# Four and three buffers for a weight conversion, and the second batch's attention products in plain float32

## The chip, the cores and the metric

The kernel runs on one core of a Trainium2 chip. The metric is the device time of one execution in microseconds (us). Three runs of the kernel before took 2249.56, 2252.94 and 2246.89 us; the median is 2249.56 us.

The engines are named as the profile names them: PE (TensorE, matmuls and transposes), PEld (its weight loads), DVE (VectorE), ACT (ScalarE), POOL (GpSimd) and SP (SyncE, which here issues every DMA). PSUM is the memory that PE writes; it is used in banks of 128 x 512 float32.

## What is computed

For 8 batches of 448 tokens with 12 heads of 64, the reference computes an attention, a spectral mix and a feed-forward block:

```python
q_n, k_n = rmsnorm(q, g_q), rmsnorm(k, g_k)
scores = q_n @ k_n.T / 8                      # 448 x 448 per head
attn = exp(scores - max) / (sum + 1e-9)
x = concat_heads(attn @ v)                    # 448 x 768 per batch
u = x + real(fft(fft(x, axis=tokens), axis=features))
un = (u - mean) / sqrt(var + 1e-6)
out = u + relu(un @ w_ch1) @ w_ch2            # 768 -> 3072 -> 768
```

The weights come as 64-bit floats and everything else as float32. The kernel reads each 64-bit number as two 32-bit words and makes two float32r numbers of it (float32r is the rounded kind that PE multiplies in fewer passes): a high part and the small rest.

## The kernel before, in words

**Two numbers for one.** A precise product is made of float32r matmuls: an operand is split into a rounded value and the rest, and two or three matmuls are summed. The split costs an ACT copy (the rounded value) and a DVE subtraction (the rest). The alternative, called plain here, feeds the float32 tile to PE as it is. A plain matmul appears in the trace as two PE records; a float32r one is one record.

**Attention of one pair of heads** (`transpose_pair`, `softmax_pair`, `value_pair`). q and k of a pair are normalised and transposed. Split, this leaves QT and KD, and the rests in the upper half of QT and in `rounded` (KL); plain, it leaves two tiles, head 0 in partitions 0 to 63 and head 1 in 64 to 127. The scores are made in four chunks of 112 rows, each head into its own PSUM bank: split, two matmuls per head (line 348); plain, one with 64 rows (line 345). After the softmax the chunks P are transposed into `pt` (line 392 plain, 420 split), copied to T, and multiplied with v into `av`, which is copied to xT. Split, v is vhl (an ACT copy and a POOL subtraction), T is split by ACT and DVE, a head needs seven matmuls (lines 432 and 437), and xT is put together by an ACT copy and a DVE addition. Plain, a head needs four matmuls (lines 399 and 403) into 64 partitions of `av`, and one copy.

Which pairs are plain stands in two ranges over the number 6 x batch + pair: the values of `PLAIN_PAIRS` and the scores of `PLAIN_SCORES`. Before, these are pairs 0 to 5 and 2 to 5, all of batch 0.

**Feed-forward** (`ffn`). `up(m)` makes one of 24 hidden tiles with 18 matmuls (line 851), `down(g, d)` one of 36 partial outputs with 12 (line 872): 864 matmuls for a batch. Each uses one weight tile of `Stream` W1 or W2, which keeps three tiles loaded and asks for the next when one was used.

**Conversion of the weights** (`convert`, `Stream.converted`). In the first pass a weight tile is loaded as 64-bit words into `dbl`, worked on, and stored to DRAM as its two float32r parts, from where the other seven batches load it. One tile is one DMA load (line 651), two ACT operations (654 and 655), three DVE operations (656, 660 and 664), a POOL addition (668), an ACT copy (669), a POOL subtraction (670) and a DMA store (700). The loaded words lie in a buffer of the tag X, the work in one of the tag M; there are two of each. 14 tiles are converted beside the attention of batch 0, the other 46 during the feed-forward of batch 0.

**Order.** `merge` interleaves the feed-forward of batch b with attention and spectral mix of batch b+1, by nominal costs that each step yields. So batch 1's attention and the 46 conversions run beside batch 0's feed-forward. A scheduler then sets the order on each engine, and every engine, SP included, works through its queue in that order. Reuse of a buffer waits for the last reader of what was in it.

Of the kernel before, what the change touches and what calls it, by code (L numbers as in the profile page):

```python
# [13 lines left out]
U32 = mybir.dt.uint32  # L14
U64 = mybir.dt.uint64
AF = mybir.ActivationFunctionType
# [3 lines left out]
B, H, S, D = 8, 12, 448, 64  # L20
DM = H * D
DFF = 4 * DM
C = 112
NC = S // C
NPAIR = H // 2
NR = DM // 128
# [15 lines left out]
CONVERT_EARLY = 0.12  # L42
EARLY = 2
DFT_STEP = 40
PLAIN_PAIRS = range(NPAIR)
PLAIN_SCORES = range(2, NPAIR)
PACE = 3
LAG = 3

# [39 lines left out]
def spectral_block(ctx, tc, q, k, v, g_q, g_k, w1, w2, d1, d2, out, nb=B):  # L89
# [49 lines left out]
    def bank(tag, name):  # L139
        if tag == "either":  # L140
            tag = ("q", "av")[turn[0] % 2]
            turn[0] += 1
        return ps.tile([128, 512], F32, tag=tag, name=name, bufs=BANKS[tag])
# [3 lines left out]
    def slot(tag, name, dtype=F32):  # L147
        return sb.tile([128, 900], dtype, tag=tag, name=name, bufs=SLOTS[tag])

    def wide(name, dtype=F32):  # L150
        return sb.tile([128, 1800], dtype, tag="X", name=name, bufs=2)
# [179 lines left out]
    def softmax_pair(b, p, Pc):  # L331
        QT, KD, _ = ready[b, p]
        for c in range(NC):
# [39 lines left out]
            Pc.append(P)  # L373
            yield 760

    def value_pair(b, p, Pc, xT):
        vhl = ready[b, p][2]
        rem = bank("PT", f"rem{b}_{p}")
# [4 lines left out]
        if plain(b, p):  # L383
            R = slot("PT", f"R{b}_{p}")[:, :S]
            A.copy(R, rem[:, :S])
            yield 420
            for h, a in enumerate((lo, hi)):
                av = bank("either" if b == 0 else "av", f"av{b}_{p}_{h}")
                for j in range(3):
                    pt = bank("PT", f"pt{b}_{p}_{h}_{j}")  # L390
                    for c in range(NC):
                        nc.tensor.transpose(
                            pt[:, c * C : (c + 1) * C],
                            Pc[c][:, 512 * h + j * 128 : 512 * h + (j + 1) * 128],
                            ident[:C, :C],
                        )
                    T = slot("PT", f"T{b}_{p}_{h}_{j}")[:, :S]
                    A.copy(T, pt[:, :S])
                    nc.tensor.matmul(
                        av[:D, :S], vhl[:, j, h], T, start=j == 0, stop=False  # L400
                    )
                    yield 1180
                nc.tensor.matmul(
                    av[:D, :S], vhl[a, 3, h], R[a], start=False, stop=True
                )
                A.copy(xT[a, p, :S], av[:D, :S])
                yield 760
            A.copy(xT[:, p, S : S + 1], xT[:, p, 0:1])
            return
# [233 lines left out]
    def convert(src, bits, part, name):  # L643
# [1 line left out]


        _, c, f = src.shape
        raw = wide(f"dbl{name}", U32)[:, : c * f].rearrange(
            "r (c f w) -> r c f w", c=c, w=2
        )  # L650
        nc.sync.dma_start(raw.rearrange("r c f w -> r c (f w)"), src)
        low, high = raw[:, :, :, 0], raw[:, :, :, 1]
        value = bits.bitcast(F32)
        behind(nc.scalar.activation(value, high.bitcast(F32), AF.Abs))
        behind(nc.scalar.activation(low, low, AF.Copy, scale=2.0**-29))
        behind(nc.vector.tensor_scalar(
            out=value, in0=value, scalar1=MIN_HIGH, scalar2=MAX_HIGH,
            op0=ALU.max, op1=ALU.min,
# [15 lines left out]
    class Stream:  # L674
# [18 lines left out]
        def converted(self, i, name):  # L693
            hl = self.tile(name)
            src = self.doubles(i)
            bits = slot("M", f"mag{self.tag}{name}", U32)[:, : self.n * 128].rearrange(
                "r (c f) -> r c f", c=self.n
            )
            convert(src, bits, [hl[:, k] for k in range(2)], f"{self.tag}{name}")
            nc.sync.dma_start(self.kept(i), hl.bitcast(F32))  # L700
            return hl
# [231 lines left out]

# [19 lines left out]
```

## Time and profile before

| | |
|---|---|
| median of three runs | 2249.56 us (2246.89 to 2252.94) |
| span of the profiled execution, first to last instruction | 2245.4 us |
| busy share of the span: PE, DVE, ACT, POOL | 94%, 72%, 47%, 24% |
| mean granted TensorE clock | 0.963 of 2.4 GHz |
| DMA moved | 425.32 MB, mean 189 GB/s |

The page gives the profiled execution's span and no time of its own beside it; the median of the runs lies 4.2 us above that span. The page cuts the span into 40 slices of about 56 us. Batch 0's attention and spectral mix fill the first 196 us; batch 0's feed-forward runs from there to about 555 us; from 555 us on each batch takes about 249 us (the 48 spectral matmuls of line 531 come at 757.28, 1006.05, 1255.05 and 1503.73 us in the chain of waits). A busy share is an average over stages with different limits, so the windows by stage below say more than the table.

### The profile page before, as it was taken

The page shows a single profiled execution, that of the slowest core. Times are in us where ns is not written, and L with a number is a line of the kernel's source. Part 1 is how long each engine was busy: PE and PEld are TensorE (multiplying, and loading weights), DVE is VectorE, ACT ScalarE, POOL GpSimd, SP SyncE. Part 2 cuts the span into 40 slices and gives each one's busy share as a digit, 9 for nine tenths or more (in the row PEclk, how much of TensorE's full clock was granted, in tenths as well). Part 3 has the DMA queues.
Part 4 walks back from the last instruction along what each step waited for, and adds up shares of the span by engine and source line. Part 5 has one row for each costly group of instructions (what it writes and reads, how often), then busy time and mean ns, then how long its engine had stood idle before and what let it go on. Part 6 is the DMA issues. An engine that isn't in the chain of part 4 may idle for free.

```text
span 2245.4 us, 31410 instructions
## 1 busy us (share of the span) xinstructions
PE 2112.2 (94%) x11164; PEld 1858.3 (83%) x11164; DVE 1617.8 (72%) x3083; ACT 1061.0 (47%) x2290; POOL 536.4 (24%) x322
## 2 busy tenths in 40 slices
PE   7877877788999999999999999999999999999997
PEld 3336766667999999999999999999999999998996
DVE  7887899877688577876888577866788587753122
ACT  6856776454454255534554255524554355422100
POOL 5763556455122012210122021211121022000000
PEclk7988988888999999999999999999999999999999
DMA  5556445577755575556655575557655675549664
GB/s 154 163 171 216 154 156 185 175 255 250 215 176 168 188 238 167 174 189 199 204 172 180 188 226 166 176 177 226 188 170 177 207 215 162 176 137 281 213 207 134
DMA packets 298238, 425.32 MB, mean 189 GB/s; under 512 B 186545, under 2 KB 224418, under 8 KB 298082
## 3 DMA queue, kind: packets, MB, share of 16 engines
q1 hardware_dynamic: 298082, 423.32, 60.4%
q8 instruction: 89, 1.46, 0.3%
q14 instruction: 67, 0.55, 0.1%
HBM read 363.47 MB, written 65.27 MB: 191 GB/s over the span
## 4 chain that ended last, share of the span: by engine, by line
PE 78%; DVE 10%; ACT 3%; DMA 3%; issue 3%; POOL 2%; SPq 0%; DVEq 0%; POOLq 0%; ACTq 0%
PE h L851 28%; PE o L872 28%; PE S L348 5%; PE av L432 4%; PE pt L420 4%; PE y L531 2%; DMA dblw<-w 2%; PE qk L311 1%; DVE mn L112 1%; DVE P L112 1%; DVE eo L112 1%; ACT P L112 1%; POOL magw L668 1%; PE oT L817 1%; DVE magw L664 1%
## 5 line engine op out<-in xcount | busy, mean ns | idle before, releaser
L872 PE MATMUL o<-hs,w 128*128 128x448 f32 x3456 | 803.7, 375 | 14.7 <-POOL w L670 4.8
L851 PE MATMUL h<-unT,w 128*128 128x448 f32 x3456 | 782.6, 371 | 3.2 <-DVE hs L112 1.9
L872 PEld LDWEIGHTS o<-hs,w 128*128 128x128 f32 x3456 | 648.5, 192 | 73.3 <-POOL w L670 7.0
L851 PEld LDWEIGHTS h<-unT,w 128*128 128x128 f32 x3456 | 643.4, 190 | 56.4 <-DVE hs L112 2.7
L112 ACT ACTIVATE P<-S,mn 112x448 f32<-112x448 f32 x384 | 243.4, 636 | 204.8 <-DVE mn L112 192.9
L112 DVE TENSOR_REDUCE mn<-S 112x1 f32<-112x448 f32 x384 | 233.3, 617 | 47.9 <-PE S L348 43.3
L112 POOL TENSOR_TENSOR qkn<-raw 112x1024 f32<-112x1024 f32 x47 | 90.4, 1924 | 718.0 <-PE qk L311 524.2
L112 ACT ACTIVATE hs<-h 128x448 fp32r<-128x448 f32 x192 | 104.4, 544 | 303.1 <-PE h L851 302.1
L112 DVE TENSOR_TENSOR acc<-o,acc 128x448 f32<-128x448 f32 x240 | 148.9, 621 | 113.8 <-PE o L872 112.4
L112 DVE SCALAR_TENSOR_TENSOR hs<-h,hs 128x448 fp32r<-128x448 f32 x192 | 119.3, 621 | 131.3 <-ACT hs L112 129.4
L432 PE MATMUL av<-T,vhl 128*128 128x448 f32 x504 | 180.0, 390 | 17.1 <-DVE T L112 8.0
L112 ACT CAST T<-pt 128x448 fp32r<-128x448 f32 x252 | 132.7, 532 | 133.1 <-PE pt L420 131.2
L112 POOL TENSOR_TENSOR ss<-ss,nhalf 112x16 f32<-112x16 f32 x48 | 148.0, 3084 | 118.5 <-DVE ss L112 117.9
L112 DVE TENSOR_TENSOR T<-pt,T 128x448 fp32r<-128x448 f32 x252 | 154.7, 618 | 27.4 <-ACT T L112 25.8
L112 DVE TENSOR_SCALAR P<-P,sm 112x448 f32<-112x448 f32 x336 | 166.1, 529 | 4.5
L348 PE MATMUL S<-KD,QT 128*112 128x448 f32 x352 | 142.7, 407 | 17.4 <-ACT P L112 9.3
L420 PE MATMUL pt<-ident,P 112*128 112x112 f32 x1008 | 144.5, 261 | 4.1 <-DVE R L112 3.1
L420 PEld LDWEIGHTS pt<-ident,P 112*128 112x128 f32 x1008 | 121.0, 142 | 25.5 <-issue 3.7
L348 PE MATMUL S<-rounded,QT 128*112 128x448 f32 x352 | 134.0, 382 | 1.8 <-DVE rounded L112 1.7
L112 POOL TENSOR_TENSOR rstd<-st,nhalf 112x1 f32<-112x1 f32 (+2 forms) x32 | 17.9, 560 | 487.6 <-DVE st L112 475.3
L432 PEld LDWEIGHTS av<-T,vhl 128*128 128x128 f32 x504 | 96.1, 193 | 28.3 <-DVE T L112 9.7
L112 DVE TENSOR_SCALAR sm<-sm 112x2 f32<-112x2 f32 x192 | 60.4, 315 | 55.3 <-ACT P L112 52.9
(122 smaller groups left out, 2613.7 us busy)
## 6 DMA issues: line engine op xcount, KB each, us to landing
w<-w SPq DMA_DIRECT2D x288, 512.0 KB, 4.3
w<-w SPq DMA_DIRECT2D x192, 768.0 KB, 4.6
dblw<-w SPq DMA_DIRECT2D x30, 512.0 KB
dblw<-w SPq DMA_DIRECT2D x16, 768.0 KB, 4.5
raw<-q SPq DMA_DIRECT2D x96, 112.0 KB, 3.5
raw<-k SPq DMA_DIRECT2D x96, 112.0 KB, 4.0
v<-v SPq DMA_DIRECT2D x96, 96.0 KB, 2.1
u_dram<-u SPq DMA_DIRECT2D x24, 336.0 KB, 4.2
```

The costliest lines, as they stand in the source:

```text
L112: ins = emit(*args, **kwargs)
L311: nc.tensor.transpose(pt[:, c * C : (c + 1) * C], qk[:, i, c].rearrange("t h d -> t (h d)"), ident[:C, :C],)
L348: nc.tensor.matmul(s_, QT[:, h, cs], K[:, h], start=step == 0, stop=step == 1)
L420: nc.tensor.transpose(pt[:, c * C : (c + 1) * C], Pc[c][:, 512 * h + j * 128 : 512 * h + (j + 1) * 128], ident[:C, :C],)
L432: nc.tensor.matmul(av[:, :S], lv, T[:, i], start=(j == 0 and i == 0), stop=False)
L531: nc.tensor.matmul(o, src[:, par, t0 : t0 + n], D1[:, ri, par, cols], start=i != 1, stop=i != 0,)
L664: behind(nc.vector.scalar_tensor_tensor(out=bits, in0=high, scalar=0xC0000000, in1=bits, op0=ALU.bitwise_and, op1=ALU.bitwise_or,))
L668: behind(nc.gpsimd.tensor_tensor(out=bits, in0=bits, in1=low, op=ALU.add))
L817: nc.tensor.transpose(op[:n, j * 128 : (j + 1) * 128], accs[b][:, 3 * half + j, t0 : t0 + n], ident,)
L851: pace(nc.tensor.matmul(o, w[:, a, c], unT[c][:, z], start=n == 0, stop=n == 17))
L872: pace(nc.tensor.matmul(o, w[:, a, f], hs[4 * g + f][:, z], start=n == 0, stop=n == 11))
```

## The change

Four things are changed. The two ranges are doubled, so that the scores and the values of all pairs of batch 1 are plain. A new function, `value_halves`, makes the plain values of batch 1: the two heads write partitions 0 to 63 and 64 to 127 of one `av` bank, head 0's matmul is held until head 1's T has been copied too, so that the two stand one behind the other in PE's queue, and one copy of 128 partitions brings both to xT. The loaded words and the work of a conversion get tags of their own, with four and three buffers, and the two ACT operations that read the loaded words change places. The program also sets `dynamic_dma_scratch_size=1024`.

```diff
@@ -42,8 +42,8 @@
 CONVERT_EARLY = 0.12
 EARLY = 2
 DFT_STEP = 40
-PLAIN_PAIRS = range(NPAIR)
-PLAIN_SCORES = range(2, NPAIR)
+PLAIN_PAIRS = range(2 * NPAIR)
+PLAIN_SCORES = range(2, 2 * NPAIR)
 PACE = 3
 LAG = 3
 
@@ -373,6 +373,42 @@
             Pc.append(P)
             yield 760
 
+    def value_halves(b, p, Pc, xT, R):
+
+        v_ = ready[b, p][2]
+        av = bank("av", f"av{b}_{p}")
+        for j in range(3):
+            T = []
+            for h in range(2):
+                pt = bank("PT", f"pt{b}_{p}_{h}_{j}")
+                for c in range(NC):
+                    nc.tensor.transpose(
+                        pt[:, c * C : (c + 1) * C],
+                        Pc[c][:, 512 * h + j * 128 : 512 * h + (j + 1) * 128],
+                        ident[:C, :C],
+                    )
+                t = slot("PT", f"T{b}_{p}_{h}_{j}")[:, :S]
+                copied = A.copy(t, pt[:, :S])
+                T.append(t)
+                yield 400
+            for h, a in enumerate((lo, hi)):
+                mm = nc.tensor.matmul(
+                    av[a, :S], v_[:, j, h], T[h], start=j == 0, stop=False
+                )
+                if h == 0:
+                    order(
+                        mm, copied,
+                        mybir.DependencyClass.Sync, mybir.DependencyReason.SCHED_ONLY,
+                    )
+            yield 800
+        for h, a in enumerate((lo, hi)):
+            nc.tensor.matmul(
+                av[a, :S], v_[a, 3, h], R[a], start=False, stop=True
+            )
+        A.copy(xT[:, p, :S], av[:, :S])
+        A.copy(xT[:, p, S : S + 1], xT[:, p, 0:1])
+        yield 800
+
     def value_pair(b, p, Pc, xT):
         vhl = ready[b, p][2]
         rem = bank("PT", f"rem{b}_{p}")
@@ -384,8 +420,11 @@
             R = slot("PT", f"R{b}_{p}")[:, :S]
             A.copy(R, rem[:, :S])
             yield 420
+            if b:
+                yield from value_halves(b, p, Pc, xT, R)
+                return
             for h, a in enumerate((lo, hi)):
-                av = bank("either" if b == 0 else "av", f"av{b}_{p}_{h}")
+                av = bank("either", f"av{b}_{p}_{h}")
                 for j in range(3):
                     pt = bank("PT", f"pt{b}_{p}_{h}_{j}")
                     for c in range(NC):
@@ -645,14 +684,13 @@
 
 
         _, c, f = src.shape
-        raw = wide(f"dbl{name}", U32)[:, : c * f].rearrange(
-            "r (c f w) -> r c f w", c=c, w=2
-        )
+        raw = sb.tile([128, 1536], U32, tag="dbl", name=f"dbl{name}", bufs=4)
+        raw = raw[:, : c * f].rearrange("r (c f w) -> r c f w", c=c, w=2)
         nc.sync.dma_start(raw.rearrange("r c f w -> r c (f w)"), src)
         low, high = raw[:, :, :, 0], raw[:, :, :, 1]
         value = bits.bitcast(F32)
+        behind(nc.scalar.activation(low, low, AF.Copy, scale=2.0**-29))
         behind(nc.scalar.activation(value, high.bitcast(F32), AF.Abs))
-        behind(nc.scalar.activation(low, low, AF.Copy, scale=2.0**-29))
         behind(nc.vector.tensor_scalar(
             out=value, in0=value, scalar1=MIN_HIGH, scalar2=MAX_HIGH,
             op0=ALU.max, op1=ALU.min,
@@ -693,9 +731,9 @@
         def converted(self, i, name):
             hl = self.tile(name)
             src = self.doubles(i)
-            bits = slot("M", f"mag{self.tag}{name}", U32)[:, : self.n * 128].rearrange(
-                "r (c f) -> r c f", c=self.n
-            )
+            bits = sb.tile(
+                [128, NR * 128], U32, tag="mag", name=f"mag{self.tag}{name}", bufs=3
+            )[:, : self.n * 128].rearrange("r (c f) -> r c f", c=self.n)
             convert(src, bits, [hl[:, k] for k in range(2)], f"{self.tag}{name}")
             nc.sync.dma_start(self.kept(i), hl.bitcast(F32))
             return hl
@@ -933,7 +971,10 @@
 
 def kernel(q, k, v, g_q, g_k, moe_w_ch1, moe_w_ch2):
     d1, d2 = dft_consts()
-    nc = bacc.Bacc("TRN2", target_bir_lowering=False, num_devices=1)
+    nc = bacc.Bacc(
+        "TRN2", target_bir_lowering=False, num_devices=1,
+        dynamic_dma_scratch_size=1024,
+    )
     ins = {
         "q": q, "k": k, "v": v, "g_q": g_q, "g_k": g_k,
         "w1": moe_w_ch1.view(np.uint64), "w2": moe_w_ch2.view(np.uint64),
```

The order of the instructions moves on every engine from batch 0's feed-forward on; in the last two thirds of PE's queue it is the same as before. Two places on PE and one on SP follow. In a name the digit behind the letters is the batch (S1 the scores of batch 1, o0 and hs0 the feed-forward of batch 0), and w1 and w2 are the two streams of weights.

PE, the scores of one chunk of a pair of batch 1 (S1_pair_chunk_head), before:

```order
L348 MATMUL S1_3_2_0_2688<-KD1_3_2346,QT1_3_2345 112x448
L348 MATMUL S1_3_2_0_2688<-rounded_66,QT1_3_2345 112x448
L311 MATMUL qk1_4_1_2853<-ident_68,qkn1_4_2661 128x112 x4
L348 MATMUL S1_3_2_1_2689<-KD1_3_2346,QT1_3_2345 112x448
L348 MATMUL S1_3_2_1_2689<-rounded_66,QT1_3_2345 112x448
```

After, another pair and chunk; two score matmuls where there were four:

```order
L910 MATMUL o0_2_0_2919<-hs0_8_2343,w2_12_2521 128x448 x3
L345 MATMUL S1_4_2_0_2907<-KD1_4_2709,QT1_4_2616 112x448
L910 MATMUL o0_2_0_2919<-hs0_9_2681,w2_12_2521 128x448 x3
L910 MATMUL o0_2_0_2919<-hs0_10_2739,w2_12_2521 128x448 x3
L910 MATMUL o0_2_0_2919<-hs0_11_2793,w2_12_2521 128x448
L345 MATMUL S1_4_2_1_2908<-KD1_4_2709,QT1_4_2616 112x448
L910 MATMUL o0_2_0_2919<-hs0_11_2793,w2_12_2521 128x448 x2
```

One plain matmul per head stands where two split ones stood. In this chunk the feed-forward's matmuls stand between the two heads. Of the 24 chunks of batch 1, 8 have the heads next to each other in the new queue and 16 have other work between them.

PE, the values (av1) of a pair of batch 1 inside a feed-forward tile, before:

```order
L872 MATMUL o0_1_3_2634<-hs0_4_1883,w2_9_2509 128x448
L872 MATMUL o0_1_3_2634<-hs0_5_2219,w2_9_2509 128x448 x3
L872 MATMUL o0_1_3_2634<-hs0_6_2315,w2_9_2509 128x448 x3
L872 MATMUL o0_1_3_2634<-hs0_7_2375,w2_9_2509 128x448 x3
L432 MATMUL av1_2_0_2532<-T1_2_0_1_2619,vhl1_2_1907 128x448
L348 MATMUL S1_3_3_1_2785<-KD1_3_2346,QT1_3_2345 112x448
L348 MATMUL S1_3_3_1_2785<-rounded_66,QT1_3_2345 112x448
L432 MATMUL av1_2_0_2532<-T1_2_0_1_2619,vhl1_2_1907 128x448
```

After, the same kind of place:

```order
L910 MATMUL o0_2_1_2960<-hs0_8_2343,w2_13_2584 128x448 x3
L910 MATMUL o0_2_1_2960<-hs0_9_2681,w2_13_2584 128x448
L395 MATMUL av1_3_2816<-T1_3_0_0_2822,v1_3_1861 64x448
L395 MATMUL av1_3_2816<-T1_3_1_0_2879,v1_3_1861 64x448
L385 MATMUL pt1_3_1_1_2953<-ident_68,P1_3_0_2399 128x112
```

Before, the two halves of T (both shown as one name) each had a matmul of 128 columns, with other work between them. Now the two heads' matmuls, 64 columns each, stand next to each other; they do so for all 18 such pairs of batch 1 (three for each of six pairs of heads).

SP, loads (dblw) and stores (w<-w) of conversions around W2's tile 18, before:

```order
L651 DMA dblw2_16_3157<-w2 128x4x256
L700 DMA w1_15_94<-w1_15_3025 128x1536
L651 DMA dblw2_17_3211<-w2 128x4x256
L700 DMA w2_2_105<-w2_15_3103 128x1024
L211 DMA raw2_3_5017<-q 112x4x64 x2
L211 DMA raw2_3_5017<-k 112x4x64 x2
L651 DMA dblw2_18_3248<-w2 128x4x256
L700 DMA w2_2_105<-w2_16_3155 128x1024
```

After:

```order
L689 DMA dblw2_18_3061<-w2 128x4x256
L738 DMA w1_14_93<-w1_14_2796 128x1536
L689 DMA dblw2_19_3104<-w2 128x4x256
L738 DMA w1_15_94<-w1_15_2861 128x1536
L689 DMA dblw2_20_3135<-w2 128x4x256
L738 DMA w2_2_105<-w2_15_2933 128x1024
L689 DMA dblw1_16_3192<-w1 128x6x256
L738 DMA w2_2_105<-w2_16_2974 128x1024
L689 DMA dblw1_17_3259<-w1 128x6x256
```

Before, the store of W1's tile 15 stands behind the load of the second tile after it in the order of conversions (W2's tiles 15 and 16). Now it stands behind the load of the fifth (W2's tile 19).

## Rows read from the trace of the kernel before

**Rows 1.** Page, 40 slices of the span: busy share in tenths.

```profile
PE   7877877788999999999999999999999999999997
DVE  7887899877688577876888577866788587753122
```

**Rows 2.** Windows: length; busy us (count) of PE, PEld, DVE, ACT, POOL; clock; DMA.

```profile
224.00:430.00 206.00, 164.91 (x783) 139.07 (x781) 191.87 (x299) 138.09 (x273) 116.03 (x68) 0.88 0.52 170
430.00:555.00 125.00, 100.51 (x448) 85.67 (x448) 97.31 (x163) 67.06 (x121) 71.95 (x49) 0.84 0.71 243
555.00:804.00 249.00, 249.00 (x1383) 228.47 (x1382) 177.40 (x361) 109.58 (x243) 33.04 (x19) 1.00 0.61 189
...
196.00:555.00 359.00, 293.41 (x1383) 250.05 (x1382) 307.03 (x498) 224.26 (x436) 196.82 (x123) 0.88 0.60 200
```

**Rows 3.** SP's own waits, 196 to 555 us: total us, times, longest.

```profile
SPq L651 <- POOL magw L668: 102.7, 37, 10.1
SPq L700 <- POOL w L670: 98.5, 44, 6.3
```

**Rows 4.** ACT's waits in the same stretch.

```profile
ACT magw L654 <- DMA dblw<-w: 25.9, 12, 3.6
...
ACT dblw L655 <- DMA dblw<-w: 12.7, 11, 2.7
```

**Rows 5.** Chain of waits, 430 to 555 us: start, us, what.

```profile
471.14 6.80 DMA dblw<-w
...
529.64 7.18 DMA dblw<-w
```

**Rows 6.** DVE groups, 196 to 555 us: xcount | busy us, mean ns | idle before.

```profile
L112 DVE TENSOR_TENSOR T<-pt,T 128x448 fp32r<-128x448 f32 x36 | 21.8, 615 | 1.3 <-ACT T L112 0.9
...
L112 DVE TENSOR_TENSOR QT<-qk,QT 64x448 fp32r<-64x448 f32 x14 | 8.7, 622 | 1.9 <-ACT QT L112 1.6
...
L112 DVE TENSOR_TENSOR rounded<-qk,KD 64x448 fp32r<-64x448 f32 x14 | 8.7, 619 | 3.5 <-ACT KD L112 3.3
...
L112 DVE TENSOR_TENSOR R<-rem,R 64x448 fp32r<-64x448 f32 x12 | 7.5, 622 | 0.4
L112 DVE TENSOR_TENSOR xT<-av,xT 64x448 f32<-64x448 f32 x12 | 7.4, 616 | 0.2
```

**Rows 7.** PE's timeline, split matmuls back to back: start us, us, line, what.

```profile
302.28 0.37 PE L348 MATMUL S<-KD,QT 128*112 128x448 f32 x1
302.48 0.36 PE L348 MATMUL S<-rounded,QT 128*112 128x448 f32 x1
```

**Rows 8.** PE's timeline, plain matmuls of batch 0 (two records each).

```profile
59.85 1.31 PE L345 MATMUL S<-KD,QT 64*112 64x448 f32 x4
61.09 0.97 PE L399 MATMUL av<-T,v 128*64 128x448 f32 x2
61.99 0.60 PE L392 MATMUL pt<-ident,P 112*128 112x112 f32 x4
62.52 1.01 PE L345 MATMUL S<-KD,QT 64*112 64x448 f32 x4
63.46 0.96 PE L399 MATMUL av<-T,v 128*64 128x448 f32 x2
...
123.61 1.00 PE L345 MATMUL S<-KD,QT 64*112 64x448 f32 x2
124.55 0.96 PE L399 MATMUL av<-T,v 128*64 128x448 f32 x2
```

**Rows 9.** POOL groups, 196 to 555 us.

```profile
L670 POOL TENSOR_TENSOR w<-magw,w 128x512 fp32r<-128x512 f32 (+1 forms) x46 | 74.3, 1620 | 51.4 <-ACT w L669 50.4 <-PE av L437 1.0
L668 POOL TENSOR_TENSOR magw<-magw,dblw 128x512 uint32<-128x512 uint32 (+1 forms) x44 | 67.6, 1537 | 85.2 <-DVE magw L664 53.7 <-DVE sm L112 12.6 <-issue 8.7
```

**Rows 10.** PE's waits, 196 to 555 us: total us, times, longest.

```profile
PE av L432 <- DVE T L112: 8.0, 5, 2.6
PE S L348 <- ACT P L112: 8.0, 6, 3.1
```

## The prediction

> **What bounds the kernel now.** The slices of the page come first [rows 1]. From the eleventh slice (561 us) to the last but one PE is at 9 tenths or more; before, it stands at 7 or 8 and DVE stands at 8 or 9 in the fifth to the eighth slice. The windows by stage put lengths to this [rows 2]. A batch in the steady part (555 to 804 us) takes 249.0 us, with PE busy in all of it at clock 1.00 and DVE in 177.4 us. That is the PE work of one feed-forward with one attention. The stage that the change touches, 196 to 555 us, has the same PE work and takes 359 us, 110 us more, at clock 0.88. It has two parts. From 224 to 430 us, beside batch 1's attention, DVE is busy 191.9 of 206 us (93%): its queue is the bound. From 430 to 555 us DVE falls to 78% and PE to 80%, and what ends last there is the conversion's data: the chain of waits has pieces of 6.80 and 7.18 us in which everything waits for a load of weights [rows 5]. The waits say why the load is late. Over the stage SP, which takes its DMAs in order, holds a load (line 651) for 102.7 us in 37 waits until POOL has read the words in one of the two buffers [rows 3], and ACT then waits 25.9 + 12.7 = 38.6 us for words that have not landed [rows 4].
>
> **The change part by part.** *DVE.* The plain path of batch 1 has no subtractions. In the stage go 36 of T (21.8 us), 12 of R (7.5), 12 additions into xT (7.4), and of QT and `rounded` 10 each: the rows count 14 for seven pairs, of which five are batch 1's and two already batch 2's, so 10 x 0.622 + 10 x 0.619 = 12.4 us [rows 6]. Together 49.1 us; DVE's 307.0 us become 258. The sixth pair's QT and `rounded`, 2.5 us, go from the stage before 196 us, whose order hardly changes and whose end I leave where it is.
>
> *PE, removed.* Split matmuls start 0.20 us apart [rows 7]. Scores: 24 chunks x 2 heads x 2 = 96; values: 6 pairs x 14 = 84; 180 x 0.20 = 36 us.
>
> *PE, added.* A plain matmul occupies PE for 0.90 us (from 61.09 to 61.99) to 0.94 us (one head's scores, from 123.61 to 124.55) [rows 8]. Two heads' scores next to each other took 0.94 us together once (62.52 to 63.46) and 1.24 us once (59.85 to 61.09). In the new order 16 of 24 chunks have their heads apart: 32 x 0.94 + 8 x 0.94 = 37.6 us, with 1.24 for the pairs 40.0. The values are 18 pairs of matmuls in two halves of the columns, and 6 pairs in two halves of rows and columns. No row shows column halves. The lower bound is the row halves' 0.94 for a pair, the upper two single matmuls, 1.80. I take the lower, since the row halves are the nearest case: 24 x 0.94 = 22.6 us. With the upper for the 18, 18 x 1.80 + 6 x 0.94 = 38.0. So PE gets 37.6 + 22.6 - 36 = +24 us, or +40 at the worse end, and the stage cannot be shorter than 249 + 24 = 273 us (or 289).
>
> The Trainium skill speaks for the lower end: its page "TensorE: Matmul & The Clock Gate", Part 3, says that matmuls in different column groups run at the same time, three of them 2.38 times as fast. It also has a rule against the change. The page "TensorEngine Tiling (Array Packing)", section Key Properties, says that changing the tiling mode drains the engine; the new order does that about 64 times (40 score and 24 value blocks), mostly among feed-forward matmuls. The rows show plain matmuls beside short transposes alone. A split matmul is 0.36 us long and the next starts after 0.20, so a drain would add up to 0.16 us a block, 64 x 0.16 = 10 us: the floor would be 283 us and, at the busy share that I use below, the time 2204 us.
>
> *Conversion.* A third and fourth buffer let SP issue loads five tiles ahead of a store instead of two. The 38.6 us that ACT waits for words should mostly go, and with them the long pieces of the chain. Its operations stay: POOL's two take 74.3 + 67.6 = 141.9 us of the stage [rows 9], which hides beside 273 us of PE. If POOL is late instead, that costs what rival 2 says. DMA moves the same bytes at a share of 0.60 over 359 us, that is 215 us of work, 0.71 of 302 us: as much as the second part has now [rows 2]. The stores still wait for POOL (98.5 us, line 700) [rows 3], and loads queue behind them on SP; with five tiles of lead this should not reach ACT. ACT and POOL also lose copies and v's split; neither is the bound (224.3 and 196.8 us busy of 359), so I cost that at nothing.
>
> *The sum.* After the change PE's 273 us is the largest content, DVE's 258 close behind. The steady stage fills PE to 1.00 with DVE at 0.71 of the length; the stage before had PE at 293.4/359 = 0.82. I take the middle, 0.90: 273/0.90 = 303 us. The ends are 273 us, all PE, and 273/0.855 = 319 us, where 0.855 is what the fuller engine, DVE, reached before (307.0/359). From 196 us on all later stages keep their order and PE-bound length, so the span falls by 359 - 303 = 56 us, from 2245.4 to 2189.4. The median of the runs stands 4.2 us above that span; so 2249.6 - 56 = 2193.6 us. By the ends: 359 - 273 = 86 gives 2163.6, 359 - 319 = 40 gives 2209.6.
>
> **The rivals.** 1. The column halves run one after the other. PE's content is 289 us; 289/0.90 = 321, a gain of 38, 2211.6 us (at 0.855: 338, 2228.6). For it: no row shows column halves side by side. Against: row halves do it.
>
> 2. The deeper buffers bring nothing, because POOL's own chain paces the tiles: POOL idles 53.7 us for DVE and 50.4 us for ACT between its two operations [rows 9], and works in order. Then the part from 430 on keeps its 125 us, and only the first shrinks: its PE content, 164.9 us at a clock of 0.88 with 24 added, lies between 0.88 x 164.9 + 24 = 169 and 189 us, so from 206 to about 179: a gain of 27, 2222.6 us. Against: both waits fall where DVE is full.
>
> 3. Slower: PE's queue stops at the plain products. Each of the 18 value pairs now waits for two copied T instead of one, and each of the 24 score chunks for two free banks, and the feed-forward queued behind cannot pass. The longest such waits before were 2.6 and 3.1 us [rows 10]. If every one came to that: 18 x 2.6 + 24 x 3.1 = 121 us, a stage of 273 + 121 = 394, 35 us slower, 2284.6 us. It decides from (359 - 273)/42 = 2.05 us a stop. Against: before, with a fuller DVE, there were only 11 such waits, 16.0 us in all.
>
> 4. No change: conversions keep their pace through the whole stage (359/46 = 7.8 us a tile), whatever DVE has to do; 2249.6 us. For it: 46 serial chains of eight operations. Against: DVE's 93% in the first part.
>
> **How the numbers follow.** My forecast has 0.53, rival 1 0.21, rival 2 0.14, rival 3 0.07, rival 4 0.05. The likeliest case alone spans 2164 to 2210. The range takes in its lower end and the worse ends of rivals 1 and 2: 2165 to 2231. About 0.3% (7 us) is what a measurement here can tell from no change. Rivals 1 and 2 are faster by more than that, so faster has 0.88, same 0.05, slower 0.07.
>
> **What would show it.** Right: the windows show the stage from batch 0's first feed-forward matmul to the end of the last conversion at about 303 us, PE at 0.9 of it, its clock up from 0.88, DVE near 258 us; ACT's waits for `dblw` a few us; SP's waits at the load line well under 102.7. Side by side or not is read from PE's timeline: two value matmuls start within some ns of each other and the pair takes 0.94 us, or the second starts 0.9 us later. Wrong: a stage over 330 us; waits of PE on copies of T or on free score banks beyond 50 us in all (rival 3); POOL's waits on ACT and DVE unchanged with the tail at 125 us (rival 2); or a change after the stage, where I expect 249 us a batch as before.

## The result, and the profile after

The changed kernel takes 2220.56 us (median of 4 runs, 2217.51 to 2221.82), the kernel before 2249.28 us in the same comparison: a ratio of 0.9874, 95% interval 0.9856 to 0.9893. It is 28.7 us faster, where 56 us were forecast. The profiled execution's span is 2215.7 us (2245.4 before).

Below, "the stage" runs from batch 0's first feed-forward product to 202.1 us before batch 2's first spectral product; in the kernel before that is 193.8 to 555.0 us, 361.2 us. In the changed kernel it is 198.2 to 524.7 us, 326.5 us. So the stage gave 34.7 us, 4.4 were lost ahead of it, and behind it almost nothing moved.

First the slices of the page (busy share in tenths, and the granted clock). They answer to [rows 1].

```profile
PE   7877998979999999999999999999999999999997
...
DVE  7876589997887587867787688857787588753122
...
PEclk8987999989999999999999999999999999999998
```

PE is now at 9 in the fifth and sixth slice, where it stood at 8 and 7; DVE has moved its 9s to the seventh to ninth slice. The windows say the same in us (length; busy us and count of PE, PEld, DVE, ACT, POOL; clock; DMA) and answer to [rows 2].

```profile
224.00:364.00 140.00, 135.41 (x616) 90.50 (x615) 107.06 (x164) 90.45 (x187) 81.92 (x49) 0.98 0.64 210
364.00:504.00 140.00, 117.32 (x571) 92.27 (x571) 134.31 (x181) 78.33 (x142) 97.25 (x55) 0.93 0.67 225
...
198.00:525.00 327.00, 298.31 (x1415) 221.34 (x1416) 272.39 (x411) 197.52 (x392) 194.68 (x116) 0.95 0.66 220
...
774.00:1023.00 249.00, 249.00 (x1395) 228.68 (x1394) 188.94 (x385) 116.67 (x262) 39.34 (x22) 1.00 0.61 189
```

The stage falls into two halves. In the first PE is full (135.4 of 140 us) and DVE has room; in the second DVE is full (134.3 of 140) and PE waits. Over the whole stage DVE's share is 272.4/327 = 0.83, yet it is nearly full in 140 us of it. In a later window of 249 us PE is busy throughout, and a batch takes as long as before: batch 3's and batch 4's first spectral products start at 977.1 and 1226.2 us, 249.1 us apart.

What PE waits for in the second half, 364 to 504 us, is mostly DVE's results: these rows are 15.4 of the 22.7 us in which it is not busy.

```profile
PE y L570 <- DVE eo L112: 5.7, 2, 5.1
PE o L910 <- DVE hs L112: 5.3, 1, 5.3
PE pt L385 <- DVE hs L112: 4.4, 1, 4.4
```

The waits on the loads: SP's own, ACT's and POOL's, 196 to 525 us (us in total, times, longest). They answer to [rows 3, 4] and to the idle times of [rows 9].

```profile
SPq L689 <- POOL magw L706: 79.7, 31, 6.5
SPq L738 <- POOL w L708: 61.8, 33, 5.3
...
ACT dblw L692 <- DMA dblw<-w: 14.2, 12, 3.4
...
POOL w L708 <- ACT w L707: 21.0, 13, 3.4
POOL magw L706 <- DVE magw L702: 19.1, 12, 5.4
```

ACT waits 14.2 us for words where it waited 38.6; SP's hold at the load falls from 102.7 to 79.7 us; POOL's waits between its two operations fall from 50.4 and 53.7 to 21.0 and 19.1 us.

PE's plain products, in its timeline (start, us, line, what; two records for each product):

```profile
256.18 2.08 PE L889 MATMUL h<-unT,w 128*128 128x448 f32 x9
258.19 1.00 PE L345 MATMUL S<-KD,QT 64*112 64x448 f32 x2
259.13 2.10 PE L889 MATMUL h<-unT,w 128*128 128x448 f32 x9
...
408.80 0.97 PE L395 MATMUL av<-T,v 128*64 128x448 f32 x4
409.71 0.97 PE L405 MATMUL av<-R,v 64*64 64x448 f32 x4
410.61 0.41 PE L416 MATMUL rem<-ident,P 112*128 112x112 f32 x2
```

The two heads' value products (four records) take 408.80 to 409.71, 0.91 us together: the column halves run side by side, as do the halves of rows and columns. One head's scores alone take 258.19 to 259.13, 0.94 us. Before a plain product there is a price: the feed-forward group ends at 256.18 + 2.08 = 258.26, its last product of 0.36 us started at 257.90, and the scores follow 0.29 us later, not 0.20. In the stage 38 plain blocks stand behind a feed-forward product, and the median of this step is 0.30 us.

Last, what nobody had priced: DVE's conversion operations beside POOL. First the groups of the kernel before (196 to 555 us: xcount | busy us, mean ns | idle before):

```profile
L656 DVE TENSOR_SCALAR magw<-magw 128x512 f32<-128x512 f32 x28 | 17.5, 624 | 15.6 <-ACT magw L654 15.4
L660 DVE TENSOR_SCALAR magw<-magw 128x512 uint32<-128x512 uint32 x28 | 15.2, 542 | 0.5
...
L112 DVE TENSOR_TENSOR qkn<-raw,ss 112x512 f32<-112x512 f32 x10 | 8.7, 907 | 0.0
```

The same groups after (196 to 525 us):

```profile
L698 DVE TENSOR_SCALAR magw<-magw 128x512 uint32<-128x512 uint32 x28 | 22.2, 793 | 0.5
L694 DVE TENSOR_SCALAR magw<-magw 128x512 f32<-128x512 f32 x28 | 20.8, 743 | 8.7 <-ACT magw L693 8.4
...
L112 DVE TENSOR_TENSOR qkn<-raw,ss 112x512 f32<-112x512 f32 x10 | 14.5, 1488 | 0.0
```

The same 28 operations on the same shape take 0.74 and 0.79 us on average, not 0.62 and 0.54. All conversion groups together, 132 operations in either stretch, went from 105.3 to 118.5 us (117.0 from the first feed-forward product on, as in the table below, with 129 of them), `qkn` from 8.7 to 14.5 us. The timeline of both engines shows how:

```profile
447.88 6.58 POOL L706 TENSOR_TENSOR magw<-magw,dblw 128x768 uint32<-128x768 uint32 x1 [5.45 <-DVE magw L702]
...
449.26 1.08 DVE L112 SCALAR_TENSOR_TENSOR eo<-eo,eo 128x900 f32<-128x900 f32 x1
...
457.60 1.84 POOL L706 TENSOR_TENSOR magw<-magw,dblw 128x768 uint32<-128x768 uint32 x1
460.39 1.87 POOL L708 TENSOR_TENSOR w<-magw,w 128x768 fp32r<-128x768 f32 x1 [0.94 <-ACT w L707]
460.52 2.69 DVE L112 SCALAR_TENSOR_TENSOR eo<-eo,eo 128x900 f32<-128x900 f32 x1
462.23 2.68 POOL L706 TENSOR_TENSOR magw<-magw,dblw 128x768 uint32<-128x768 uint32 x1
463.14 2.72 DVE L112 TENSOR_TENSOR eo<-eo,eo 128x900 f32<-128x900 f32 x1
465.78 1.08 DVE L112 TENSOR_TENSOR tot<-tot,eo 128x900 f32<-128x900 f32 x1
465.85 2.68 POOL L708 TENSOR_TENSOR w<-magw,w 128x768 fp32r<-128x768 f32 x1 [0.94 <-ACT w L707]
```

DVE's operation of 128x900 takes 1.08 us at 449.26 and at 465.78, where it stood ahead of POOL's or POOL was already held up. At 460.52 it starts 0.13 us after one of POOL's, which ends at 460.39 + 1.87 = 462.26, and ends itself 0.95 us after that: 2.69 us. The next begins while POOL works again, until 462.23 + 2.68 = 464.91, and again ends 0.95 us later. In the last two rows DVE was first, and POOL's 1.87 us became 2.68. POOL's addition, 1.84 us at 457.60, took 6.58 at 447.88 beside a dense stretch of DVE. Whoever is second waits for the first to end. The Trainium skill says the same, on its page "SBUF — State Buffer", section "Who interferes with whom": the two engines have one pair of ports in common, taken for a whole instruction, and issue order decides who blocks. The trace agrees.

### The profile page after: what moved, and what is told of

It reads as the page before. It is cut to its first block, busy times and chain, and to the rows that moved or that the text cites. A ratio compares the mean times of both kernels' runs of the same rounds, so it can differ in the third digit from the quotient of the medians.

```text
span 2215.7 us, 31224 instructions
## 1 busy us (share of the span) xinstructions
PE 2117.6 (96%) x11176; PEld 1822.6 (82%) x11176; DVE 1583.1 (71%) x2999; ACT 1033.6 (47%) x2248; POOL 533.6 (24%) x316
## 4 chain that ended last, share of the span: by engine, by line
PE 77%; DVE 11%; DMA 4%; ACT 3%; issue 3%; POOL 2%; SPq 0%; DVEq 0%; POOLq 0%; ACTq 0%
PE h L889 28%; PE o L910 28%; PE S L348 5%; PE av L471 4%; PE pt L459 4%; PE y L570 1%; DMA u_dram<-u 1%; DMA w<-w 1%; PE qk L311 1%; DVE P L112 1%; DVE sm L112 1%; DVE mn L112 1%; DVE magw L702 1%; DVE magw L694 1%; POOL magw L706 1%
## 5 line engine op out<-in xcount | busy, mean ns | idle before, releaser
L910 PE MATMUL o<-hs,w 128*128 128x448 f32 x3456 | 793.6, 372 | 12.0 <-DVE hs L112 7.2
L910 PEld LDWEIGHTS o<-hs,w 128*128 128x128 f32 x3456 | 640.4, 190 | 76.4 <-issue 10.7
L112 DVE SCALAR_TENSOR_TENSOR hs<-h,hs 128x448 fp32r<-128x448 f32 x192 | 119.3, 621 | 128.1 <-ACT hs L112 126.4
L112 ACT CAST T<-pt 128x448 fp32r<-128x448 f32 x216 | 113.6, 532 | 125.5 <-PE pt L459 123.3
L112 DVE TENSOR_TENSOR T<-pt,T 128x448 fp32r<-128x448 f32 x216 | 132.8, 618 | 31.4 <-ACT T L112 30.1
L471 PE MATMUL av<-T,vhl 128*128 128x448 f32 x432 | 151.8, 382 | 0.0
L459 PE MATMUL pt<-ident,P 112*128 112x112 f32 x864 | 121.3, 259 | 0.0
L348 PE MATMUL S<-KD,QT 128*112 128x448 f32 x304 | 119.2, 394 | 1.8 <-ACT KD L112 1.7
L459 PEld LDWEIGHTS pt<-ident,P 112*128 112x128 f32 x864 | 102.6, 140 | 16.4
L348 PE MATMUL S<-rounded,QT 128*112 128x448 f32 x304 | 113.6, 376 | 1.8 <-DVE rounded L112 1.7
L706 POOL TENSOR_TENSOR magw<-magw,dblw 128x512 uint32<-128x512 uint32 (+1 forms) x46 | 78.7, 1710 | 58.3 <-DVE magw L702 19.1
## 6 DMA issues: line engine op xcount, KB each, us to landing
raw<-q SPq DMA_DIRECT2D x96, 112.0 KB, 4.1
raw<-k SPq DMA_DIRECT2D x96, 112.0 KB, 3.4
```

Source lines behind the costliest of these rows:

```text
L112: ins = emit(*args, **kwargs)
L348: nc.tensor.matmul(s_, QT[:, h, cs], K[:, h], start=step == 0, stop=step == 1)
L459: nc.tensor.transpose(pt[:, c * C : (c + 1) * C], Pc[c][:, 512 * h + j * 128 : 512 * h + (j + 1) * 128], ident[:C, :C],)
L471: nc.tensor.matmul(av[:, :S], lv, T[:, i], start=(j == 0 and i == 0), stop=False)
L706: behind(nc.gpsimd.tensor_tensor(out=bits, in0=bits, in1=low, op=ALU.add))
L910: pace(nc.tensor.matmul(o, w[:, a, f], hs[4 * g + f][:, z], start=n == 0, stop=n == 11))
```

## The experiments

All ran in groups beside the kernel before (2248.9 to 2249.2 us). The table has each kernel's median and ratio to before; when the first feed-forward product starts; the length of the stage; PE's and DVE's busy time in it; and DVE's conversion operations from that start on. Runs of one kernel lie 0.6 to 8 us apart. All keep the changed kernel's own tags for the conversion and its `dynamic_dma_scratch_size`, so what these two do is not shown. An edit also moves the order that the scheduler sets on every engine; each difference is that of the edit and its new order together.

| kernel | us | ratio (95%) | starts | stage | PE | DVE | conv. |
|---|---|---|---|---|---|---|---|
| before | 2249.3 | 1 | 193.8 | 361.2 | 295.6 | 308.2 | 105.3 |
| changed | 2220.6 | 0.9874 (.9856-.9893) | 198.2 | 326.5 | 298.0 | 272.2 | 117.0 |
| two buffers | 2239.1 | 0.9956 (.9941-.9971) | 197.1 | 349.1 | 304.2 | 272.1 | 104.8 |
| buffers only | 2234.8 | 0.9935 (.9921-.9950) | 205.5 | 338.8 | 278.6 | 312.4 | 117.0 |
| values, one head | 2236.1 | 0.9943 (.9928-.9958) | 201.0 | 343.0 | 314.3 | 277.5 | 125.2 |
| heads together | 2215.0 | 0.9844 (.9827-.9860) | 202.9 | 319.7 | 284.7 | 273.6 | 114.4 |
| scores split | 2212.3 | 0.9836 (.9822-.9851) | 201.2 | 318.8 | 281.9 | 290.0 | 121.8 |
| no rest on POOL | 2192.7 | 0.9750 (.9733-.9766) | 195.9 | 304.3 | 289.1 | 234.5 | 88.8 |
| value first | 2210.8 | 0.9828 (.9812-.9845) | 196.4 | 322.3 | 297.6 | 264.3 | 112.0 |
| scores split, value first | 2207.7 | 0.9816 (.9801-.9831) | 193.7 | 320.5 | 278.8 | 284.2 | 114.2 |
| one DVE op less | 2204.4 | 0.9799 (.9782-.9816) | 198.9 | 317.0 | 293.4 | 246.8 | 85.3 |
| value first, scaling on ACT | 2206.7 | 0.9814 (.9799-.9829) | 194.1 | 319.3 | 296.4 | 251.7 | 112.2 |
| together, value first, scaling on ACT | 2202.8 | 0.9797 (.9783-.9812) | 197.2 | 314.6 | 284.8 | 256.2 | 115.1 |
| split, value first, scaling on ACT | 2202.3 | 0.9787 (.9763-.9810) | 193.0 | 317.6 | 282.4 | 271.8 | 126.4 |

**1. The plain products with two buffers.**

```
-  tag="dbl", ..., bufs=4        +  bufs=2
-  name=f"mag{...}", bufs=3      +  bufs=2
```

> The changed kernel with two buffers each, instead of four and three, for the loaded words and for the work of a conversion; batch 1 stays plain. Theory A (both parts are needed: with two buffers the conversions wait for their loads again, but DVE is still relieved): 2230 to 2242 us, ACT's waits for loaded words back near 30 us. Theory B (the forecast's rival 2, deeper buffers bring nothing): 2217 to 2224 us, as with the deeper buffers. Theory C (the plain products give PE what they take from DVE, so alone they bring nothing): 2244 us or more.

2239.1 us, as theory A had it. The plain products give 9.9 us without the deeper buffers. The swap of ScalarE's two operations is still in this kernel, and in the next. ACT waits for words again:

```profile
ACT dblw L692 <- DMA dblw<-w: 32.4, 18, 4.6
```

**2. The buffers alone.**

```
-PLAIN_PAIRS = range(2 * NPAIR)       +PLAIN_PAIRS = range(NPAIR)
-PLAIN_SCORES = range(2, 2 * NPAIR)   +PLAIN_SCORES = range(2, NPAIR)
...                                   (the split values in their banks of before)
```

> Four and three buffers, with batch 1's scores and values split as in the kernel before. Theory A (both parts are needed): 2230 to 2242 us, DVE full beside batch 1's attention (about 300 us busy from the first feed-forward matmul to the end of the conversions). Theory B (deeper buffers bring nothing): 2245 to 2252 us. Theory C (the buffers bring all of it): 2217 to 2224 us.

2234.8 us, again as theory A had it and 14.2 less than before, so rival 2, "the deeper buffers bring nothing", falls. Alone the parts give 9.9 + 14.2 = 24.1 us, together 28.7: they nearly add up, with the swap, which run 8 finds to cost time, in both. DVE has 312.4 us in a stage of 338.8 here, 0.92; it is the fuller engine, and its conversion operations are at 117 us already.

**3. Both heads' plain scores given to PE together.** Head 0's product waits until the last exponential has left the banks, as head 1's does; in the order 23 of 24 chunks then have their heads next to each other, not 8.

```
+ if b and h == 0 and freed:
+     order(mm, freed[-1], Sync, SCHED_ONLY)
...
+ if tag == "S": freed.append(done)     # done: the exponential
```

> The changed kernel with head 0's plain score matmul of batch 1 held until head 1's bank is free too, so that 23 of 24 chunks have their two heads next to each other in PE's queue. PE loses about 14 to 17 us of content (some 15 blocks of 0.93 us with 0.1 us of switching). Theory A (PE is the bound for the first 160 us of the stage, DVE after that): 5 to 10 us faster than the change, 2210 to 2216 us. Theory D (DVE alone bounds the stage after the change): no change, 2218 to 2224 us. Against both: head 0's later start delays the softmax, 2224 us or more.

2215.0 us, 5.5 us better than the change. PE's busy time falls by 13 us and DVE's changes by 1, as theory A had it: PE's time counted.

**4. The second batch's scores split again, its values plain.**

```
-PLAIN_SCORES = range(2, 2 * NPAIR)   +PLAIN_SCORES = range(2, NPAIR)
```

> The changed kernel with batch 1's scores split as before; only its values are plain, side by side. PE loses about 20 us of content in the stage (24 chunks at 0.82 instead of mostly 1.87 us), DVE gets 12.4 us and ACT some 11 us back. Theory A (PE and DVE about equally full): within 5 us of the change, 2215 to 2226 us. Theory E (PE bounds the stage): 2203 to 2212 us. Theory D (DVE bounds the stage): 2228 to 2236 us.

2212.3 us: 8.3 us better than the change, though DVE got 17.8 us more; PE has 16.1 us less. The plain scores, most of them one head at a time, were a part of the change that cost time. The time lies 0.3 us beyond the end of theory E's range and 3 us below theory A's: PE's relief counted for more than DVE's load, and by more than A allowed.

**5. The second batch's plain values one head at a time.**

```
-            if b:
-                yield from value_halves(b, p, Pc, xT, R)
-                return
...              # each head's product into a bank of its own, as before
```

> The second batch's value products stay plain float32, but each head has its own bank and its own turn, so 48 products of 64 rows run alone instead of 24 side by side. The changed kernel's trace has a side-by-side block at 0.90 us and a lone plain product at 0.93 to 0.94 us, so PE gets about 48 x 0.93 - 24 x 0.90 = 23 us more; DVE and POOL get nothing. Theory A (PE is the tighter engine in the stage in which both batches overlap): the time rises by 15 to 25 us, to 2235 - 2246 us, and PE's share of the stage stays near 0.86. Theory D (DVE and the conversion chain are the tighter ones, PE has room): the time rises by at most 8 us, to 2221 - 2229 us, and PE's share of the stage rises above 0.90.

2236.1 us, 15.5 us slower than the change, with PE's busy time up by 16.3 us: theory A on the time. PE's share of the stage stays, at 0.92 after 0.91, though not near the 0.86 that the text names. DVE also has 5.3 us more, which neither theory had, and two copies bring a pair to xT where one did. So most of what makes the plain values pay is running side by side.

**6. Without POOL's subtraction.** The rests of the weights are left out (ScalarE writes a copy of the value in their place).

```
-behind(nc.gpsimd.tensor_tensor(out=part[1], in0=value, in1=part[0], op=ALU.subtract))
+behind(nc.scalar.copy(part[1], value))
```

> Leaves out POOL's subtraction (the rest of each weight after rounding): ScalarE writes a copy of the value there instead, so POOL has one operation for each chunk and the weights' rests are not those of the reference. Theory S (DVE's conversion operations are long because POOL works at the same time: in the changed kernel 128x512 takes 0.72 us beside POOL and 0.42 alone): DVE's operations of the conversion fall from 117 us in sum to 85 - 105, the mean of the 128x512 one towards 0.5 - 0.6 us, DVE's busy time in the stage from 272 to about 250 - 262. Theory L (their length has to do with something else, the deeper buffers or the shape): the sum stays at 112 - 120 us. On the time: if PE is the tighter engine (A) 2208 - 2219 us, if DVE is (D) 2198 - 2210 us; ScalarE gets some 15 to 20 us more and has 125 us idle in the stage.

2192.7 us, 27.9 us less than the change, which is more than either theory had on the time. The windows of its stage, and its DVE groups:

```profile
196.00:500.00 304.00, 288.86 (x1397) 215.10 (x1398) 234.18 (x401) 219.89 (x431) 114.77 (x68) 0.97 0.72 236
```

```profile
L694 DVE TENSOR_SCALAR magw<-magw 128x512 f32<-128x512 f32 x27 | 13.9, 513 | 4.1 <-ACT magw L693 2.9 <-POOL magw L706 1.2
L698 DVE TENSOR_SCALAR magw<-magw 128x512 uint32<-128x512 uint32 x27 | 12.3, 457 | 0.3
L112 DVE TENSOR_TENSOR qkn<-raw,ss 112x512 f32<-112x512 f32 x12 | 10.5, 911 | 0.9 <-POOL ss L112 0.8
```

With POOL at 114.8 us instead of 194.7, DVE's operations shrink from 743 to 513, from 793 to 457 and from 1488 to 911 ns (the shift on 128x768 alone grew, from 719 to 1006), and DVE has 38 us less in the stage. 28 of them are the conversion's, without one of its 129 operations gone; some 5 are `qkn`'s, and the rest goes with 9 other operations fewer in the shorter stage. PE fills 288.9/304 = 0.95 of the stage. This is theory S on the lengths; on the time it leaves open what was DVE's and what POOL's own.

**7. One DVE operation of the conversion left out** (the shift of the bits) with POOL's work kept, to tell these apart.

```
-behind(nc.vector.tensor_scalar(out=bits, in0=bits, scalar1=5, scalar2=2,
-    op0=ALU.logical_shift_left, op1=ALU.logical_shift_right))
```

> Leaves out one of VectorE's three operations of the conversion (the shift of the bits, so the weights are not those of the reference): in the changed kernel about 44 of them between 196 and 525 us, 22.2 us for the 28 of 128x512 and some 16 us for the 16 of 128x768, 38 us of DVE's 272 us in the stage. POOL keeps all its work. It tells what the 28 us came from that the run without POOL's subtraction gained: theory D (DVE's time, which fell by 38 us there, also by 38 here): 2190 - 2202 us, and PE's share of the stage rises from 0.91 to 0.94 or more. Theory Q (POOL's own time, which fell by 99 us there and stays here): at most 8 us are gained, 2212 - 2221 us, and POOL stays at 250 us or more. A time between says that both count.

(No row shows the 99 and 250 us of POOL in that text; by the windows it fell by 80 us in run 6 and has 185.2 us here. The shifts are not 38 us either: those on 128x768 take 11.5 us in the changed kernel, not 16, and all of them in its stage 33.3.) 2204.4 us, 16.2 us less: between the theories, so both count. PE's share of the stage rises to 0.93, short of the 0.94 of theory D. DVE lost 25.4 us and not 33.3, in part since three of the four groups of the conversion that stayed got longer; the fourth, the first operation on 128x768, got shorter (1146 to 800 ns). Two of the three:

```profile
L698 DVE SCALAR_TENSOR_TENSOR magw<-dblw,magw 128x512 uint32<-128x512 uint32 x27 | 28.9, 1073 | 0.6
L694 DVE TENSOR_SCALAR magw<-magw 128x512 f32<-128x512 f32 x27 | 23.2, 858 | 5.8 <-ACT magw L693 5.6
```

(L698 is here the last of the three, L702 in the changed kernel, where it took 941 ns.) That is 16.2/25.4 = 0.64 us of time for 1 us of DVE. At that rate the 37.8 us of run 6 are worth some 24 of its 27.9 us. This is an estimate: DVE and POOL can't be changed apart, and run 7 also shortens each tile's chain by one operation, which the rate puts down to DVE.

**8. ScalarE's two operations in the order of before,** and **9. the same with split scores.**

```
-behind(nc.scalar.activation(low, low, AF.Copy, scale=2.0**-29))
 behind(nc.scalar.activation(value, high.bitcast(F32), AF.Abs))
+behind(nc.scalar.activation(low, low, AF.Copy, scale=2.0**-29))
```

> Undoes one small part of the change: ScalarE computes the value of a chunk before it scales the low half again, instead of after. Theory O (this order, in which the loads are waited for by the first of the two, costs the 4 to 5 us that the first feed-forward product starts late): it starts at 194 - 196 us instead of 198 and the time is 2214 - 2218 us. Theory N (the late start comes from the plain products of batch 0's pairs and when the scores are given to PE): it starts at 197 - 200 us and the time is within 3 us of the changed kernel's, 2217 - 2223 us.

> The second batch's scores as split products again (as in the run with scores split, 2212 us), and ScalarE's two operations in the order of before. Theory O (ScalarE's order costs time): 2206 - 2210 us. Theory N (it doesn't matter): 2210 - 2215 us.

2210.8 us, 9.8 us better than the change: theory O's direction, and more than it allowed. With split scores 2207.7 us, 4.5 us better than run 4: theory O as well. This small swap was part of the change, and a second part that cost time. In the trace of run 8 the first product starts 1.8 us earlier, the stage is 4.2 us shorter and DVE has 7.9 us less; DVE's first operation on a chunk needs the value alone and no longer waits for the scaling (0.9 us on 128x768). Which wait turns that into 9.8 us isn't shown. It need not be one: PE's order in run 8 differs from the changed kernel's from its 147th record on, 813 of 11176 records stand elsewhere, and no run keeps the order and swaps the two alone.

**10. The second batch's scaling all on ScalarE,** on top of run 8; **11.** with the heads' scores together as well; **12.** on top of run 9.

```
-if b < EARLY and h == 0:      +if b < EARLY and (h == 0 or b):
     A.activation(Ph[h], Ph[h], AF.Copy, scale=sm[:, h : h + 1])
```

> The order of ScalarE's two operations of before, and for the second batch the scaling of both heads' exponentials on ScalarE instead of one head's on VectorE: 24 operations, of 0.80 us on DVE (19 us off its 264) and 0.68 us on ACT (16 us onto its 195). Nothing of the result changes. Against the run with ScalarE's order alone (2211 us): theory D (DVE holds the second part of the stage): 2199 - 2206 us. Theory A (PE holds it): 2207 - 2212 us. Theory L (ScalarE answers later, and the scores' banks come free later): 2213 us or more.

> All that helped at once, with the result of the reference: the plain scores of two heads given to PE together, ScalarE's two operations in the order of before, the second batch's scaling on ScalarE. The parts gained 5.5 us (heads together) and 10 us (order) by themselves. If they add up, and the scaling gives 5 more, 2198 - 2202 us; if they take the same time away (both start from the late first feed-forward product), 2204 - 2210 us.

> The run with split scores and ScalarE's order of before (2208 us) with the second batch's scaling on ScalarE as well: DVE 284 us in that run's stage, less 24 x 0.80 = 19 us. There PE has 279 us and DVE 284 us, so if each holds its part of the stage in turn, relief of DVE is worth more here than where PE has 298 us and DVE 264 us (4 us, from 2211 to 2207 us). Theory D: 2196 - 2203 us. Theory A (PE alone, the same 4 us or less): 2203 - 2208 us.

Run 10: 2206.7 us, 4.1 us better than run 8, in the gap between D's range and A's; 12.6 us less on DVE gave 4.1, a rate of 0.33. Run 12: 2202.3 us, 5.4 us better than run 9 for 12.4 us, 0.44: theory D on the time. That the rate is higher where DVE has more than PE is not shown, as the two gains differ by 1.3 us and the runs of one kernel by up to 5.7 here. Run 11: 2202.8 us, 0.8 us beyond the range for parts that add up. Its three parts gave 5.5, 9.8 and 4.1 us by themselves, 19.4 together, and 17.8 at once: they nearly add up. Runs 11 and 12 keep the reference's computation and are the best of such versions, 46 to 47 us faster than before; they can't be told from each other.

## Why the prediction was right in its direction and wrong in its size

The mechanism was right: DVE relieved, column halves side by side, loads further ahead, the clock up from 0.88 to 0.95, nothing lost behind the stage. The size was not. The time, 2220.6 us, lies outside the forecast's own 2164 to 2210, and the stage of 326.5 us lies just under the 330 from which on the prediction called itself wrong. The time is inside the stated range only because that took in the worse ends of rivals 1 and 2, and both fall below; that part was luck.

**DVE's removals, right as far as they went; the step that failed is what was left.** The step said "DVE's 307.0 us become 258" and kept every remaining duration. Measured are 272.4. The conversion's groups grew by 13.2 us and `qkn` by 5.8, 19 together, of which a shorter stage with less of batch 2 in it hides some. The deeper buffers let POOL work in more of the time in which DVE does, and each blocks the other: POOL is busy in 0.54 of DVE's busy time before, in 0.58 with two buffers, in 0.61 with the buffers alone, in 0.62 in the changed kernel. In the run with two buffers the conversion stays at 104.8 us; with the buffers alone it has its 117. `qkn` is another matter. It grew with the plain products and not with the buffers, as its rows in run 1 (two buffers) and run 2 (buffers alone) show, beside 907 ns before:

```profile
L112 DVE TENSOR_TENSOR qkn<-raw,ss 112x512 f32<-112x512 f32 x10 | 12.1, 1250 | 0.8 <-POOL ss L112 0.8
L112 DVE TENSOR_TENSOR qkn<-raw,ss 112x512 f32<-112x512 f32 x10 | 6.5, 678 | 0.0
```

**PE's terms, nearly right.** The rows of the trace give 0.91 us for a value block and 0.94 for a lone score product, against 0.94 and 0.94 in the sum. The 0.10 us before a block (0.30 where split products start 0.20 apart) stands in the place of the drain that was weighed at 0.16 at most: about 52 blocks of the timeline stand behind another kind of product, 5 us. So PE's content was some 249 + 24 + 5 = 278 us (an estimate), not 273, half way to the 283 us that 64 full drains would have made (283/0.90 is 314 us and gives 2205 us, not the 2204 of the prediction). The Trainium skill's rule is that changing the tiling mode drains the engine ("TensorEngine Tiling (Array Packing)", Key Properties). The trace agrees that such a change costs time, 0.10 us of it. That the scores apart were dear was in the sum, and that they were not worth it was not seen: 16 chunks apart cost 32 x 0.94 us where runs 3 and 4 show a way without them.

**Rival 1 (column halves in turn) falls** by the timeline, **rival 3** by the waits on banks and copies, whose rows answer to [rows 10]:

```profile
PE S L345 <- ACT P L112: 2.8, 3, 1.3
...
PE av L395 <- ACT T L112: 0.7, 1, 0.7
```

3.5 us, not 121. **Rival 2** falls by run 2, and by the last part of the stage: from 430 us on, 125 us became 95. **Rival 4** falls with the result.

**The conversion, half right.** ACT's waits for words fell by 24.4 of 38.6 us. SP's hold at the load fell less than said, by 23 of 102.7 us: POOL still frees the buffers, only later ones.

**The sum, the term that was off.** "I take the middle, 0.90: 273/0.90 = 303 us." Measured, PE's content fills 278/326.5 = 0.85 of the stage, at the lower end that was taken from DVE's share before. The windows show the reason. An average share hides that the bound changes hands within the stage: PE is full in the first half and DVE in the second, where PE waits for DVE; an average of both shows room that neither half has. Of the stage's 326.5 us PE was not busy in 28.5, most of it in the second half. The other 298.0 stand against a content of 278. By the clock in the trace PE was busy for 25.5 us at the lower of its two levels, 1.2 GHz, where feed-forward products start 0.37 us apart instead of 0.20; that costs some 12 us (an estimate). The last 8 us stay open.

**Two edits at nothing.** The swap of ScalarE's operations had no term in the sum; run 8 puts 9.8 us on it and the order that comes with it. And the step that left 196 us, "whose end I leave where it is", moved 4.4 us late.

So 27 us of the 56 went missing. In the terms of the sum they are 4.4 us before the stage, 5.6 for PE's content at 0.90 (278/0.90 = 309 us, not 303) and 17.6 for the fill (326.5 us, not 309); the stage before was 361.2 us and not 359, which takes 2 back, and the rest is under 2 us. Of what stands behind the start and the fill, run 8 finds 9.8 us, and the conversion's and `qkn`'s 19 us on DVE at 0.64 are worth some 12 (an estimate from run 7). The two overlap, as run 8 has 7.9 us less on DVE, and can't be added. Runs 3 and 4 gain 5.5 and 8.3 us but explain none of this, since the plain scores' cost stood in the sum. Runs 11 and 12, without the swap, with the scores together or split, and with some DVE work on ScalarE, come within some 9 us of the forecast.

## What to carry to other kernels

Where two engines are each near full, find the half of the stage in which each one is full before dividing a content by an average share. Durations read beside an idle neighbour don't hold when the change lets that neighbour work more: look for the same operation short and long in the trace of before, and ask what ran beside the long ones. In the trace of before DVE's 128x900 stands at 1.08 us and twice at 2.69. Price every line of a diff, also a swap of two operations, and undo the parts one by one: here two parts out of four, the plain scores and the swap, cost time.

## What the runs showed of the hardware

A DVE operation with two inputs of 128x900 took 1.08 us by itself and 2.7 us when one of POOL's had started before it; POOL's addition took 1.84 us and, behind DVE, up to 6.58. Taking POOL's busy time from 195 to 115 us shortened the 129 conversion operations of DVE by 28 us in sum without taking one away, and taking one kind of operation from DVE made three of the four conversion groups that stayed longer (743 to 858 ns for one of them). Two plain float32 products in column halves of PE run side by side, 0.91 us for both, and going over to them from a split product costs about 0.10 us.
